# One core, attention into a gated MLP: a weight load in two, scores by two units earlier, two output copies on ScalarE, and gated work moved past unit 36

## The chip, the core and the metric

The kernel runs on one core of a Trainium2 chip. The metric is device time in microseconds: the median of several runs. Before the change it is 239.21 us (238.92, 239.21 and 239.23). TensorE (PE) multiplies matrices into eight PSUM banks, ScalarE (ACT) and VectorE (DVE) read these and write to SBUF, GpSimd (POOL) works on SBUF alone, and SyncE (SP) only issues transfers. Transfers are also issued from the queues of ACT and POOL.

## The reference

Grouped-query attention over 8 batches, whose output is the input of a gated MLP with a spatial mix over the 384 positions:

```python
k = np.repeat(k, group, axis=1); v = np.repeat(v, group, axis=1)   # 4 -> 16 heads
scores = scale * np.matmul(q, k.transpose(0, 1, 3, 2))              # 8 x 16 x 384 x 384
scores = scores - np.max(scores, axis=-1, keepdims=True)
attn = np.exp(scores)
attn = attn / (np.sum(attn, axis=-1, keepdims=True) + 1e-09)
x = np.matmul(attn, v)                                             # heads side by side: 8 x 384 x 1024
...
h = np.maximum(x @ w_in, 0.0)                                      # 1024 -> 1024
u, v = h[..., :512], h[..., 512:]
v_n = (v - mean(v)) / np.sqrt(var(v) + 1e-06)
v_s = np.einsum('ts,bsd->btd', w_spatial, v_n) + b_spatial[None, :, None]
return (u * v_s) @ w_out                                           # 512 -> 1024
```

All inputs and the output are float32. The kernel computes in float16 with float32 sums.

## The kernel before

**Two streams on one TensorE.** The kernel's order of instructions is written out by hand. The attention stream is a row of 144 units, 18 for each batch (`UNITS`). A unit is one block of 128 keys for one set of heads and queries; three units make a set, six sets a batch. `units` (L264) multiplies keys by queries into two PSUM banks for a unit (one for each half `hh`, the tile `sc`), and `exp` (L288) is two ScalarE activations from these to `aT`. When the three units of a set are done, `weigh` (L292) multiplies by v (tile `av`, 12 matmuls for a half), and VectorE takes the reciprocal of the sums and scales (`r`, `x`). For batch 0, x is transposed on TensorE (`x_turn`, L324, tile `xps`, copied by VectorE to `xt`); later batches send it through a transposing transfer on SyncE's queue (`x_send`, L334).

**The gated stream** is a generator (`gated`, L487). It yields the MLP's matmuls one by one, each with its cost: `v_part` (tile `pv`, eight matmuls of 512 columns), `u_part` (`pu`, 32 of 384), `s_part` (`psp`, 12 of 384) and `o_part` (`po`, four of 512 for each half of an output tile). It also yields marks `("from", n)`: nothing behind the mark may come before unit n. `pour` (L696) takes matmuls from it as long as some time is owed, and returns 0 at a mark that isn't reached. `o_part` copies each half from PSUM to `osb` on VectorE or ScalarE (`copy`, L214), and SyncE stores the whole.

**The main loops.** The first (L718 to 737) runs over units 0 to 20 (`ALONE`): one unit at a time up to unit `TWO` - 1, then two at a time; it carries out what `at(n, ...)` has put down for that unit (turns, casts, loads), then the `weigh` that is due, then pours as much gated work as the unit has to spare (`spare`, 736 ns, or 600 and 870 for two). The second (L743 to 765) runs over groups of three units from 21 on. Each has `share` of gated work, cut into four pieces (`F`) between scores, exponentials and `weigh`.

**Banks.** `bank` (L77) gives each tile the PSUM bank which, by a rough clock kept while the program is built, comes free first.

**Queues.** GpSimd's queue carries the loads that cast (`load_w_in`, L159, `load_w_out`) and several loads of q, k, v, in order among its casts (`cast_q`, L194; `cast_v`, L187; `cast_k`). SyncE's queue carries the other loads, the transposing sends (`k_send`, `q_send`, `x_send`) and the stores, in program order, each waiting there for what it needs. At L581 to 618 the first loads and casts are laid out, at L656 to 662 those of batch 2.

Of the kernel before, what the change touches and what calls it, by code (L numbers as in the profile page):

```python
# [17 lines left out]
def kernel(  # L18
# [51 lines left out]
    pool, dve, act, sp = nc.gpsimd, nc.vector, nc.scalar, nc.sync  # L70
# [14 lines left out]
    def spend(ns):  # L85
        clock[nc.tensor] += ns
# [42 lines left out]
    def load_q(b, j, eng=sp, ts=(0, 1, 2)):  # L129
        if ts[0] == 0:  # L130
            stage_tile("q", b, j)
        part_q(b, j, (0, 1), ts, eng)
# [26 lines left out]
    def load_w_in(half, lo, hi):  # L159
        cols = slice(half * DH, (half + 1) * DH)  # L160
        pool.dma_start(
            w_in16[:, lo:hi, cols],
            moe_w_in[lo * P : hi * P, cols].rearrange("(t p) f -> p t f", p=P),
        )
# [29 lines left out]
    def cast_q(b, j, eng, ts=None, hs=(0, 1)):  # L194
        if (b, j) not in q16s:
            q16s[b, j] = ld.tile([P, NT, G, 2, D], FP16, name=f"q16_{b}_{j}", tag="q16", bufs=4)
        t16 = q16s[b, j]
        src = stage["q", b, j].rearrange("p h t (r d) -> p h t r d", d=D)
        for hh in hs:
            if ts is None:  # L200
                eng.tensor_copy(t16[:, :, :, hh, :], src[:, hh])  # L201
            elif len(ts) > 1:
                t = slice(ts[0], ts[-1] + 1)
                eng.tensor_copy(t16[:, t, :, hh, :], src[:, hh, t])
            else:
                eng.tensor_copy(t16[:, ts[0], :, hh, :], src[:, hh, ts[0]])  # L206
# [249 lines left out]
    def o_part(b, tt, half):  # L456
        last = b == B - 1
        if half == 0:
            osbs[b, tt] = ops.tile([P, DM], FP32, name=f"osb_{b}_{tt}", tag="osb")
        osb = osbs[b, tt]  # L460
        rows = out[b].rearrange("(p t) d -> p t d", t=NT)

        parts = [(half * 512, 512, act if half and (last or tt == 1) else dve, sp)]
        if last and tt == NT - 1 and half:
            parts = [(512, 384, dve, sp), (896, 128, act, act)]
        for c0, width, eng, queue in parts:
            po = bank([P, 512], FP32, f"po_{b}_{tt}_{c0}")
            for m in range(NM):
                nc.tensor.matmul(  # L469
                    po[:, 0:width],  # L470
                    gTs[b][:, m, tt * P : (tt + 1) * P],
                    w_out16[:, m, c0 : c0 + width],
                    start=(m == 0),
                    stop=(m == NM - 1),
                )
                spend(C512 * width / 512)
                if m < NM - 1:
                    yield C512 * width / 512
            cols = slice(c0, c0 + width)
            copy(eng, osb[:, cols], po[:, 0:width], f"po_{b}_{tt}_{c0}")  # L480
            if last:
                queue.dma_start(rows[:, tt, cols], osb[:, cols])
            elif half:
                sp.dma_start(rows[:, tt, :], osb)
            yield C512 * width / 512
# [77 lines left out]
    def at(n, f, *args):  # L563
        todo.setdefault(n, []).append((f, args))
# [14 lines left out]
            nc.tensor.matmul(ps, zero16, zero16, start=True, stop=True)  # L579

    cast_k(0, pool, (0,), slice(1, 2))  # L581
    load_w_in(1, 0, 4)
    cast_k(0, dve, (0,), slice(0, 1))
    cast_q(0, 0, dve, (0,), (0,))
    cast_q(0, 0, dve, (0,), (1,))
# [13 lines left out]
    def behind_rest():  # L599
        load_q(1, 1, pool)  # L600
        load_v(1, pool)
        cast_q(0, 1, pool, (2,))
        load_w_in(0, 0, 4)
        load_w_in(0, 4, 8)
        new_spatial()
        pool.memset(spatial32["b"][:, 0:1], 0.0)
        pool.memset(spatial32["w"][:, 0, 0:1], 0.0)
        load_spatial(sp)
        cast_k(1, pool)
        load_k(2, pool)  # L610
        cast_q(1, 0, pool)
        load_q(2, 0, pool, (0,))
        cast_q(1, 1, pool, (0,))
        cast_q(1, 1, pool, (1, 2))
        load_q(2, 1, pool, (0,))
        cast_v(1, pool)
        cast_spatial()
        send_spatial()
# [34 lines left out]
    at(26, q_send, 2, 1, 0, 1)  # L653
    at(26, load_w_out, 0, DH)
    at(26, load_w_out, DH, DM)
    at(29, load_q, 2, 0, sp, (1, 2))  # L656
    at(29, load_v, 2)
    at(31, load_q, 2, 1, sp, (1, 2))
    at(36, cast_v, 2, pool)
    for j, n in ((0, 34), (1, 36)):  # L660
        at(n, cast_q, 2, j, pool, (1, 2))
        at(n + 1, q_send, 2, j, 1, NT)
# [25 lines left out]
    STEP = (NT * NK * C512 + NM * NK * C384 + NM * NT * C384 + 6 * NM * C512) / SETS  # L688
# [7 lines left out]
    def pour(n, owed):  # L696
        while owed > 0:
            if n < wait_for[0]:
                return 0.0
            x = next(fill, None)  # L700
            if x is None:
                return 0.0
            if isinstance(x, tuple):
                wait_for[0] = x[1]
            else:
                owed -= x
        return owed
# [6 lines left out]
    F = (0.2, 0.3, 0.1, 0.4)  # L714
    owed = 0.0
    halves = {}
    TWO = 13
    for u in range(ALONE):  # L718
        if u < TWO or (u - TWO) % 2 == 0:
            pairs = units(u, 1)  # L720
            if u >= TWO and u + 1 < ALONE:
                pairs += units(u + 1, 1)
            for pair in pairs:
                exp(*pair)
        spare = 736 if u < TWO else (600 if (u - TWO) % 2 == 0 else 870)
        for f, args in todo.pop(u, []):
            f(*args)
            spare -= 224 if f in (q_turn, x_turn, k_turn) else 0
        for b, s in ends.pop(u, []):
            halves.setdefault(u, []).append((b, s, 0))  # L730
            halves.setdefault(u + (0 if s == 0 else 1), []).append((b, s, 1))
        for h in halves.pop(u, []):
            weigh(*h)
            spare -= 372
            if h[2]:
                turn_x(*h[:2], u)
        owed = pour(u, min(owed, 0) + spare)
    for u in sorted(halves):
        for h in halves[u]:
            weigh(*h)  # L740
    owed = 0.0
    late = [(b, s, hh) for u in (ALONE, ALONE + 1) for b, s in ends.pop(u, []) for hh in range(2)]
    for n in range(ALONE, total, NT):  # L743
        share = STEP * (0.85 if n < 90 else 1.0)
        exps = units(n, NT)
        for pair in exps[:NT]:
            exp(*pair)
        owed = pour(n, owed + share * F[0])
        for h in late:
            weigh(*h)  # L750
            if h[2]:
                turn_x(*h[:2], n)
        owed = pour(n, owed + share * F[1])
        for u in range(n, n + NT):
            for f, args in todo.pop(u, []):
                f(*args)
        for pair in exps[NT:]:
            exp(*pair)
        owed = pour(n, owed + share * F[2])
        late = []  # L760
        for u in range(n, n + NT):
            for b, s in ends.pop(u + 2, []):
                weigh(b, s, 0)
                late.append((b, s, 1))
        owed = pour(n, owed + share * F[3])
# [36 lines left out]
```

## Time and profile before

| What | us |
|---|---|
| median of three runs | 239.21 |
| the profiled execution | 238.38 |
| its span (first to last instruction) | 236.4 |
| TensorE busy | 230.1 |
| ScalarE busy | 169.5 |
| VectorE busy | 142.7 |
| GpSimd busy | 101.5 |
| first scores on TensorE | 5.74 |
| first group of three units (21 to 23) | 27.56 |
| last `av`, then gated work alone | 202 |

Times within the program are us from the start of the span. Busy time of TensorE is taken from modelled ends, since matmuls are pipelined: the start of one matmul to the start of the next is the better measure, and the prediction uses it. The other engines' rows have real starts and durations. The granted TensorE clock is 1.00 in every stretch. The share of the DMA engines is about 1.1 from 6 to 85 us and falls behind that to 0.8 and below.

### The profile page before, as it was taken

What the parts mean: (1) busy time and instruction counts of PE and PEld (TensorE: products, weight loads), DVE (VectorE), ACT (ScalarE), POOL (GpSimd) and SP (SyncE); (2) the same over time, 40 slices, a digit from 0 to 9 for tenths busy, and PEclk for the clock granted to TensorE, in tenths of its full rate; (3) what the DMA queues carried; (4) which work ended last, traced back from release to release, by engine and by line L of the source; (5) the groups of instructions that cost most, each with busy time, mean ns of one, the idle gap of its engine ahead of it and who ended that gap; (6) DMA issues with size and microseconds to landing.
All of it is one profiled execution on the core that took longest, in us unless ns stands there. A gap on an engine that the chain in (4) does not pass through costs nothing.

```text
span 236.4 us, 5917 instructions
## 1 busy us (share of the span) xinstructions
PE 230.1 (97%) x2312; PEld 123.6 (52%) x2312; DVE 142.7 (60%) x379; ACT 169.5 (72%) x348; POOL 101.5 (43%) x145
## 2 busy tenths in 40 slices
PE   7899999999999999999999999999999999999993
PEld 6455655545554546544564545555465455545541
DVE  2568774676457764566646576376744667367362
ACT  2999989969997869977797776986697776401211
POOL 3669583651464543275045800575022500460550
PEclk9999999999999999999999999999999999999999
DMA  6999979999998999899989899389912643240147
GB/s 196 273 305 320 272 143 178 212 266 260 259 227 208 260 372 192 228 200 318 193 239 224 234 202 302 63 281 158 257 26 44 114 155 89 49 177 0 68 200 267
DMA packets 67467, 47.47 MB, mean 201 GB/s; under 512 B 48336, under 2 KB 60416, under 8 KB 67440
## 3 DMA queue, kind: packets, MB, share of 16 engines
q1 hardware_dynamic: 62512, 39.86, 69.4%
q0 software_dynamic: 3952, 6.42, 12.2%
q10 hardware_dynamic: 976, 0.82, 1.1%
q8 instruction: 18, 0.29, 0.5%
q14 instruction: 9, 0.07, 0.1%
HBM read 25.95 MB, written 12.58 MB: 163 GB/s over the span
## 4 chain that ended last, share of the span: by engine, by line
PE 93%; DVE 2%; DMA 2%; issue 0%; ACTq 0%; ACT 0%
PE pu L412 18%; PE pv L353 18%; PE po L469 18%; PE sc L278 15%; PE av L298 15%; PE psp L431 7%; DMA q<-in_q_dram 2%; PE qps L238 1%; PE xps L330 1%; DVE x L313 1%; DVE osb L216 1%; DVE qT L216 0%; DVE q L206 0%; DVE r L311 0%; DVE vr L367 0%
## 5 line engine op out<-in xcount | busy, mean ns | idle before, releaser
L290 ACT ACTIVATE aT<-sc 128x512 f16<-128x512 f32 x288 | 147.7, 612 | 31.0 <-PE sc L278 30.3
L298 PEld LDWEIGHTS <-aT 128*128 128x128 f16 x1152 | 47.0, 97 | 17.0 <-issue 2.1
L353 PE MATMUL pv<-w_in,xt 128*128 128x512 f16 x192 | 51.0, 380 | 0.1
L298 PE MATMUL av<-v,aT 128*128 128x65 f16 x1152 | 50.5, 193 | 0.0
L469 PE MATMUL po<-w_out,gT 128*128 128x512 f16 (+2 forms) x196 | 50.5, 375 | 0.0
L412 PE MATMUL pu<-xt,w_in 128*128 128x384 f16 x256 | 49.9, 326 | 0.0
L397 POOL TENSOR_SCALAR vn<-vr,rstd,nmr 128x512 f16<-128x512 f32 x23 | 17.7, 783 | 66.7 <-DVE nmr L392 45.3
L448 POOL TENSOR_TENSOR gT<-vs,uT 128x384 f16<-128x384 f32 x31 | 32.5, 1058 | 31.8 <-DVE r L311 16.9
L313 DVE TENSOR_TENSOR x<-av,r 128x256 f16<-128x256 f32 x96 | 40.7, 424 | 3.3
L278 PE MATMUL sc<-qT,kT 64*128 64x512 f16 x288 | 41.6, 380 | 0.4 <-DVE qT L216 0.2
L311 DVE RECIPROCAL r<-av 128x4 f32<-128x4 f32 x96 | 17.1, 179 | 40.4 <-PE av L298 40.1
L216 DVE COPY osb<-po 128x512 f32<-128x512 f32 (+1 forms) x39 | 26.6, 683 | 17.3 <-PE po L469 17.2
L412 PEld LDWEIGHTS <-w_in 128*128 128x128 f16 x256 | 22.1, 98 | 17.1 <-issue 5.5
L423 ACT ACTIVATE uT<-pu 128x384 f16<-128x384 f32 x32 | 15.8, 495 | 16.0 <-PE pu L412 15.8
L469 PEld LDWEIGHTS <-gT 128*128 128x128 f16 x196 | 17.4, 98 | 17.3 <-issue 3.2
L353 PEld LDWEIGHTS <-xt 128*128 128x128 f16 x192 | 15.8, 97 | 17.8 <-issue 6.0
L278 PEld LDWEIGHTS <-kT 64*128 64x128 f16 x288 | 10.9, 94 | 23.7 <-issue 12.1
L431 PE MATMUL psp<-wsT,vn 128*128 128x384 f16 x96 | 22.2, 327 | 0.0
L443 DVE TENSOR_TENSOR vs<-psp,bias_bc 128x384 f32<-128x384 f32 x32 | 17.6, 552 | 7.0 <-PE psp L431 6.9
L201 POOL CAST q<-q 128x768 f16<-128x768 f32 x22 | 17.6, 831 | 9.2 <-DMA q<-in_q_dram 4.5
L367 DVE TENSOR_SCALAR vr<-pv 128x512 f32<-128x512 f32 x24 | 16.4, 683 | 8.4 <-PE pv L353 8.3
L379 DVE BATCH_NORM_STATS2 stats<-vr 128x6 f32<-128x512 f32 x24 | 16.4, 685 | 0.1
(47 smaller groups left out, 98.9 us busy)
## 6 DMA issues: line engine op xcount, KB each, us to landing
out_dram<-osb SPq DMA_DIRECT2D x21, 512.0 KB, 3.2
q<-in_q_dram SPq DMA_DIRECT2D x10, 768.0 KB, 5.8
v_None<-in_v_dram SPq DMA_DIRECT2D x6, 384.0 KB, 5.8
w_in<-in_moe_w_in_dram POOLq DMA_DIRECT2D x4, 512.0 KB, 9.8
k_None<-in_k_dram SPq DMA_DIRECT2D x5, 384.0 KB, 4.0
q<-in_q_dram POOLq DMA_DIRECT2D x2, 768.0 KB, 8.4
out_dram<-osb SPq DMA_DIRECT2D x5, 256.0 KB, 2.2
w_out<-in_moe_w_out_dram POOLq DMA_DIRECT2D x2, 512.0 KB, 8.5
```

The source lines that it names most:

```text
L201: eng.tensor_copy(t16[:, :, :, hh, :], src[:, hh])
L216: (act.copy if eng is act else dve.tensor_copy)(o, i)
L278: nc.tensor.matmul(sc, kTs[b][rows, j, kt * P : (kt + 1) * P], qTs[b, j][rows, qt].rearrange("p (r i c) -> p i r c", r=G, i=G), start=True ...
L290: act.activation(a, sc, AF.Exp, scale=scale)
L298: nc.tensor.matmul(av[:, i * (D + 1) : (i + 1) * (D + 1)], aT[:, kt, hh, i * P : (i + 1) * P], v1[b % 2][:, 2 * j + hh, kt, 0 : D + 1], st ...
L313: dve.tensor_tensor(x16s[b][:, qt, c : c + 256].rearrange("p (i d) -> p i d", i=G), o[:, :, 0:D], r.to_broadcast([P, G, D]), ALU.mult,)
L353: nc.tensor.matmul(pv, xts[b][:, kt, st * P : (st + 1) * P], w_in16[:, kt, DH:DFF], start=(kt == 0), stop=(kt == NK - 1),)
L397: (dve if b == 0 and st == 1 else pool).tensor_scalar(vn, v_r.pop((b, st)), rstd[:, st : st + 1], nmr[:, st : st + 1], op0=ALU.mult, op1=A ...
L412: nc.tensor.matmul(pu[:, 0:S], w_in16[:, kt, m * P : (m + 1) * P], xts[b][:, kt, :], start=(kt == 0), stop=(kt == NK - 1),)
L431: nc.tensor.matmul(psp[:, 0:S], v_n[b, st][:, m * P : (m + 1) * P], wsT16[:, st, :], start=(st == 0), stop=(st == NT - 1),)
L448: pool.tensor_tensor(gT, vs, uT, ALU.mult)
L469: nc.tensor.matmul(po[:, 0:width], gTs[b][:, m, tt * P : (tt + 1) * P], w_out16[:, m, c0 : c0 + width], start=(m == 0), stop=(m == NM - 1),)
```

## The change

Six edits. The first load of w_in's second half of columns is issued as two transfers. Units go by two from unit 11 instead of 13. In the first loop the transposes of x are put down behind the gated work poured for that unit. Two copies of output halves, (batch 0, tile 1, half 0) and (batch 1, tile 0, half 0), go from VectorE to ScalarE. In groups that start before unit 36 the share of gated work is 0.8 of a step instead of 0.85. And the loads and casts of q and v are moved: the cast of batch 1's first q in two with a load between, v of batch 2 loaded before q on SyncE's queue and cast at unit 33 instead of 36.

```diff
-        parts = [(half * 512, 512, act if half and (last or tt == 1) else dve, sp)]
+        by_act = half and (last or tt == 1) or (b, tt, half) in ((0, 1, 0), (1, 0, 0))
+        parts = [(half * 512, 512, act if by_act else dve, sp)]
...
-    load_w_in(1, 0, 4)
+    load_w_in(1, 0, 2)
+    load_w_in(1, 2, 4)
...
-        cast_q(1, 0, pool)
+        cast_q(1, 0, pool, (0,))
         load_q(2, 0, pool, (0,))
+        cast_q(1, 0, pool, (1, 2))
...
+    at(29, load_v, 2)
     at(29, load_q, 2, 0, sp, (1, 2))
-    at(29, load_v, 2)
     at(31, load_q, 2, 1, sp, (1, 2))
-    at(36, cast_v, 2, pool)
+    at(33, cast_v, 2, pool)
...
-    TWO = 13
+    TWO = 11
...
+        turns = []
         for f, args in todo.pop(u, []):
-            f(*args)
+            if f is x_turn:
+                turns.append(args)
+            else:
+                f(*args)
             spare -= 224 if f in (q_turn, x_turn, k_turn) else 0
...
         owed = pour(u, min(owed, 0) + spare)
+        for args in turns:
+            x_turn(*args)
...
-        share = STEP * (0.85 if n < 90 else 1.0)
+        share = STEP * (0.8 if n < 36 else 0.85 if n < 90 else 1.0)
```

## The prediction

> **What bounds the kernel now.** I read the page's summary and its chain of waits first, then the timeline of the stages that the diff touches, then the wait before each long gap of the chain.
>
> ```profile
> PE 230.1 (97%) x2312; PEld 123.6 (52%) x2312; DVE 142.7 (60%) x379; ACT 169.5 (72%) x348; POOL 101.5 (43%) x145
> ...
> PE 93%; DVE 2%; DMA 2%; issue 0%; ACTq 0%; ACT 0%
> ```
>
> TensorE is the chain, and the granted clock is 1.00 throughout, so a gain must be TensorE time. I took the start-to-start times of its matmuls: a 512-column one follows another after 216 ns, a 384-column one after 162, the narrow `av` ones after 29. What lies above these, and above 0.32, 0.54 and 0.75 us for blocks of two, four and six `sc` (from the first to the next other matmul), is lost: behind the first loads 0.54 us at 10.5 to 11.4, 0.18 at 22 to 23, 0.73 at 27.6 to 31.9, 0.10 at 54.1, 0.60 at 54.4, 0.09 at 69.0, 0.16 at 80.8, 0.12 at 100.1, 0.15 at 205.2: 2.7 us. No gain but a saved switch can be larger.
>
> The switch: from 16.36 a `pv` of 216 ns is followed by `sc` only after 0.31 us, and `sc` by `av` after 0.32 us instead of 0.216.
>
> ```profile
> 16.36 0.38 PE L353 MATMUL pv<-w_in,xt 128*128 128x512 f16 x1
> 16.67 0.39 PE L278 MATMUL sc<-qT,kT 64*128 64x512 f16 x2
> 16.99 0.54 PE L298 MATMUL av<-v,aT 128*128 128x65 f16 x12
> ```
>
> So each block of scores costs 0.09 + 0.10 = 0.19 us beyond its columns. ScalarE is as tight here: its row runs without a gap.
>
> ```profile
> 6.15 15.32 ACT L290 ACTIVATE aT<-sc 128x512 f16<-128x512 f32 x30 [1.34 <-PE sc L278]
> ...
> 21.70 6.11 ACT L290 ACTIVATE aT<-sc 128x512 f16<-128x512 f32 x12 [0.23 <-PE sc L278]
> ```
>
> The largest later loss, and the stage that causes it (the second view is of busy time by stretch: us, PE, PEld, DVE, ACT, POOL, clock, DMA):
>
> ```profile
> 54.42 1.30 PE L278 MATMUL sc<-qT,kT 64*128 64x512 f16 x6
> ...
> 54.68 0.10 PEld L278 LDWEIGHTS <-kT 64*128 64x128 f16 x2 [0.17 <-DVE x L313]
> ...
> 55.13 0.10 PEld L278 LDWEIGHTS <-kT 64*128 64x128 f16 x2 [0.36 <-issue]
> ```
>
> ```profile
> 47.90:52.07 4.17, 4.17 (x43) 2.03 (x42) 3.07 (x8) 3.05 (x6) 2.82 (x5) 1.00 1.06 294
> 52.07:54.41 2.34, 2.34 (x34) 1.34 (x33) 1.13 (x6) 1.85 (x4) 0.35 (x1) 1.00 1.15 133
> ```
>
> This block of six takes 1.35 us to the next work (55.77) instead of 0.75. The 0.10 before it is the last `av` waiting for its exponential. The group before is only 2.34 us long, against six exponentials of 0.51 us (3.05): the gated stream had stopped at its "not before unit 42" mark, so the scores of unit 42 came before ScalarE had emptied their PSUM banks.
>
> **The change, part by part.**
>
> **Units by two from 11.** Units 11 and 12 share one block: one switch fewer, -0.19 us. The shares 600 + 870 replace 2 x 736, and I add up the owed sum: units 10, 11, 12 get 1, 1, 2 `pv` instead of 1, 2, 1, and every later unit as before. ScalarE follows, because its gap of 0.23 at 21.70 is a wait for `sc`: it has 0.23 to give, 0.19 is taken.
>
> **x turned behind gated work.** Only where the unit pours something does the order change. By the same sums units 5, 9, 15 and 18 pour nothing at their end, so only unit 12 differs: four transposes (4 x 56 ns) go behind two `pv` (432 ns). `x` of its second half would be finished about 0.3 us after the transposes' old place in the new order (`av` 0.37, reciprocal 0.18 and multiply 0.42 on VectorE); the two `pv` hide it. Cost 0, and 0.3 without that cover.
>
> **Less gated work up to unit 36.** One share is 2916 ns; 0.05 of it in four groups (24 to 33; at 21 the stream stands at its mark) is 583 ns. Stepping through the shares matmul by matmul, the old order comes out as in the trace, and the new one is three `pv` (648 ns) behind at the end of group 36 and catches all of it up in group 39, which pours six `pv` instead of three. From unit 42 the order is the same. No work goes away; group 39 grows from 2.34 to 2.99 us, about the 3.05 that ScalarE needs, so the 0.60 and the 0.10 should close: -0.70. What is late next: the groups of units 27 and 30 shrink by 0.32 and 0.16 us. The first holds 4.17 us of ScalarE work in 4.41, so it is full: between 0 and +0.2; I take +0.1.
>
> **Two copies on ScalarE.** Rows: VectorE 0.69 us, ScalarE 0.59 to 0.64. The copy of (1,0,0) is what holds the bank here:
>
> ```profile
> 80.44 0.67 DVE L216 COPY osb<-po 128x512 f32<-128x512 f32 x1
> 80.78 0.10 PEld L298 LDWEIGHTS <-aT 128*128 128x128 f16 x1
> 81.16 0.52 PE L298 MATMUL av<-v,aT 128*128 128x65 f16 x12
> ```
>
> ScalarE idles 1.01 us before 80.07, so there the copy is done by about 80.25: -0.16. The copy of (0,1,0) meets a ScalarE with 3.70 us of 4.16; with 0.64 it is 4.34, and runs 0.2 into group 54, which has 3.04 of 4.07. Its own loss of 0.09 at 69.0 may go; the `av` of group 54, 0.75 us behind its exponentials now, would stand about level with them. -0.1 to +0.3; I take 0.
> The Trainium skill (ScalarE: Activation LUTs, Rules for kernel authors) speaks against such a move: simple element work belongs on VectorE, and ScalarE costs about 0.3 us plus 0.83 ns per element, an estimate of 0.72 us here. This trace disagrees for a copy out of PSUM (0.59 to 0.64 beside 0.69); by the page the sum would be 0.1 us worse at most.
>
> **First w_in load in two.** One more GpSimd issue of 0.75 us (row at 8.20), put into GpSimd's idle 4.57 to 7.03, where it waits for k; the second load still issues at 8.20. The first half is needed at 13.01 and landed, whole, at 12.19 by the landing events. Cost 0; if the cover went, see the last rival.
>
> **Third v sooner, cast_q split.** The split adds 0.32 us of GpSimd (two casts of 0.38 and two of 0.585 for 1.60) ahead of a 2.48 us wait for the spatial weights: 0. `v` of batch 2 was cast until 49.95, needed at 50.54; the new order needs it at about 50.1, so the move protects 0.2 us. Its price: on SyncE v (384 KB) goes before q, so q lands near 49.0 instead of 47.84; on GpSimd the cast of v stands before the cast of q. The cast of q (1.17) then ends near 50.0 (was 49.07), and behind it in SyncE's queue stand q's transposing send (49.09, now 50.0, 1.23 us of issue), `x_send` of batch 1's last third (50.78, now 51.2), k and q loads of batch 3. `x_send` landed 3.84 us after issue: 55.1; its `pv` would come at 54.9 (55.77 less 0.19, 0.70). Bounds: 0 (`x_send` as early as now) to +1.2 (v as late as now, 49.0, both casts behind it, `x_send` landing at 56.1); v, issued first, should land 1 to 2 us before that, so +0.2.
>
> **Sum.** -0.19 - 0.70 - 0.16 + 0.1 + 0 + 0.2 = -0.75. The profiled execution took 238.38 (span 236.4 and 2.0 around it), 0.8 under the median of 239.21. Off the median: **238.5 us**.
>
> **Rivals.**
>
> **Loads take the gain (239.3).** For: the DMA share is 1.0 and more up to 85 us, so landings don't follow TensorE; q of batch 3 landed at 70.59 for scores at 71.52, and its slack of 0.93 falls to 0.18. Against: `x_send` issues earlier when x is earlier. If v lands at 49.0, the `pv` of unit 42 waits 1.2: -0.95 without its term becomes +0.2, and the rest is lost there. Chance 0.18.
>
> **More goes (237.8).** ScalarE's 0.1 and SyncE's 0.2 don't arise, and of the 0.73 at 27.6 to 31.9 (transposes and scores that wait for banks) some 0.3 goes, as the planner gives the banks out anew: -1.35. Against: nothing in the diff aims there. Chance 0.12.
>
> **The back half of w_in comes late (239.8).** Mechanism: GpSimd's queue carries one more transfer ahead of the load of k tiles 4 to 7; that load landed at 16.25 and its first `pv` started at 16.36, a slack of 0.11. If a hole as between the w_out issue (33.37) and its first packet (34.83), 1.46 us, opens between the halves, TensorE stands still 1.35 us there: +1.35 - 0.75 = +0.6. It decides from a landing past about 17.1. Against: the packets of that queue began at 7.41, long after the issue, behind the other loads, so a hole of issue is covered. Beside it, the Trainium skill (DMA: Bandwidth & Descriptors, Anatomy of one DMA, and Rules for kernel authors) gives each such transfer a fixed 2.0 us and advises fewer, larger ones; taken serially that would be a stall of 1.9 us, and about 240.3. The trace, with transfers landing 1.2 to 2.4 us apart under load, shows them overlapped. Chance 0.13.
>
> **That nothing changes** because order and banks stay is ruled out by the sums above.
>
> **How the numbers follow.** Forecast 238.5, chance 0.57, its own range 238.1 to 238.9. What a measurement of this kernel can tell from no change is about 0.2%, 0.48 us: faster means under 238.73. Faster: 0.47 of the 0.57, all 0.12, 0.03 of the 0.18: 0.62. Slower (above 239.69): 0.12 of the 0.13 and 0.05 of the loads, where they cost 0.3 more: 0.17. Within: 0.21. Range over all: 237.8 to 239.7.
>
> **What would show it.** Right: scores of units 11 and 12 as one row of four near 16.7; group 39 near 3.0 us, and six scores after it in 0.8; no gap before `av` near 80. Wrong: a gap before `pv` at 16.4, before `pv` of unit 42 (near 55), or before the scores of unit 54 (near 70.8, where q lands), or new bank waits on ScalarE in groups 27 to 33 and 51 to 54.

## The result, and the profile after

The changed kernel takes **239.50 us** (median of 22 runs, 238.47 to 242.06). The kernel before, run beside it on the same chip, takes 238.77 (22 runs, 237.98 to 240.37). The ratio is 1.0042, with a 95% interval of 1.0026 to 1.0058: 1.0 us slower by the ratio and 0.73 by the two medians, where 0.75 us faster was forecast. The ratio leaves out the one run after, 242.06, that is over 1.5% above the fastest of its kernel. The median of 239.21 from which the forecast was counted came from three runs; 22 put it at 238.77, so 0.4 us of the distance between 238.5 and a sum made on 238.77 is the starting point. The sign is not.

It is no even shift. The lowest runs lie 0.5 us apart, but 7 of the 22 runs after are above 240 us, against 2 of 22 before.

And part of it lies outside the span. Device time is the span, from the first instruction to the last, and what lies around it. In the 111 runs of the kernel before whose spans are on record (those of the experiments), 1.96 to 2.14 us lie around the span; in the changed kernel it is 2.42 by the median, and over 2.2 in 18 of its 22 runs. So some 0.4 us of the loss is no wait of TensorE, and no row of a timeline shows it: the instructions of the trace all lie within the span.

The profiled execution of the changed kernel took 239.24 (span 236.8), 0.86 above that of before. First its summary: busy time of each engine, and the shares of the chain of waits by engine.

```profile
PE 229.8 (97%) x2312; PEld 123.8 (52%) x2312; DVE 141.6 (60%) x377; ACT 170.0 (72%) x350; POOL 102.5 (43%) x148
...
PE 87%; DMA 9%; POOL 1%; DVE 1%; SPq 1%; issue 0%
```

TensorE has the same 2312 matmuls. But it was 93% of the chain, and is 87%; transfers went from 2% to 9%. So transfers now stand where TensorE waits, though a share of the chain isn't a price. To place and price the waits, I take the start of the first scores of each unit and subtract the same start in the profile before (negative is sooner; units in `exp` order):

| unit, start before | 10, 15.41 | 11, 16.67 | 13, 18.98 | 36, 47.90 | 39, 52.08 | 45, 59.13 | 51, 67.35 | 54, 71.52 | 63, 83.92 | last, 197.29 |
|---|---|---|---|---|---|---|---|---|---|---|
| after | -0.48 | +0.07 | -0.14 | -0.57 | -0.79 | -0.06 | -0.06 | +0.50 | +0.48 | +0.49 |

A lead of 0.48 from sooner first loads is lost before unit 11; 0.21 is won by unit 13; between units 27 and 39 scores run ahead, as gated work is poured later; by unit 45 that is paid back, and more; before unit 54 0.56 goes at one stroke. Nothing happens behind unit 63. The places, in the timeline of the changed kernel (start, us, engine, line, operation, output<-inputs, count, in brackets the idle time before and what ended it):

```profile
16.43 0.38 PE L353 MATMUL pv<-w_in,xt 128*128 128x512 f16 x1 [0.39 <-DMA w_in<-in_moe_w_in_dram]
16.74 0.60 PE L278 MATMUL sc<-qT,kT 64*128 64x512 f16 x4
...
54.19 1.07 PE L278 MATMUL sc<-qT,kT 64*128 64x512 f16 x6
55.70 0.61 PE L353 MATMUL pv<-w_in,xt 128*128 128x512 f16 x2 [0.43 <-DMA xt<-x]
...
72.02 0.82 PE L278 MATMUL sc<-qT,kT 64*128 64x512 f16 x6 [0.54 <-DMA qT<-q]
...
81.64 0.53 PE L298 MATMUL av<-v,aT 128*128 128x65 f16 x12
```

At 16.43 the first `pv` that needs the second w_in load stands still, and 0.55 us go between units 10 and 11 (its load landed at 16.39, at 16.25 before). At 16.74 units 11 and 12 do share a row of four `sc`. From 54.19 the six scores of unit 42 take 1.51 us to the next work, not 0.75; the timeline puts the last part of that down to `x_send`'s transfer. At 72.02 the scores of unit 54 wait for batch 3's q.

Busy time by stretch for groups 36 and 39 (us, PE, PEld, DVE, ACT, POOL, clock, DMA share, GB/s), to be read against the 4.17 and 2.34 of before:

```profile
47.33:51.29 3.96, 3.96 (x42) 1.93 (x43) 2.68 (x8) 3.05 (x6) 2.15 (x4) 1.00 0.95 310
51.29:54.19 2.90, 2.90 (x37) 1.67 (x37) 1.85 (x5) 2.42 (x6) 1.18 (x2) 1.00 0.82 122
```

Group 39 grew to 2.90, as forecast (2.99). What stood behind the forecast's +0.2 is seen in SyncE's queue, before and then after (start, duration of the issue):

```profile
42.77 1.46 SPq L122 DMA_DIRECT2D q<-in_q_dram  x1
44.29 0.45 SPq L112 DMA_DIRECT2D v_None<-in_v_dram  x1
...
49.09 1.23 SPq L256 DMA_TRANSPOSE qT<-q  x1
50.78 1.23 SPq L337 DMA_TRANSPOSE xt<-x  x1
```

```profile
42.77 1.44 SPq L112 DMA_DIRECT2D v_None<-in_v_dram  x1
44.27 0.49 SPq L122 DMA_DIRECT2D q<-in_q_dram  x1
...
50.31 2.10 SPq L256 DMA_TRANSPOSE qT<-q  x1
52.51 1.25 SPq L337 DMA_TRANSPOSE xt<-x  x1
```

q of batch 2 lands at 49.06 instead of 47.84, its two casts on GpSimd start at 49.11 instead of 47.90, so the transposing send starts 1.22 later, and its issue takes 2.10 instead of 1.23. The send of x behind it starts 1.73 later and lands at 55.65 (54.62 before). The q load of batch 3 is issued at 55.81 (54.55 before), and its transposed tile lands at 71.88, not 70.58: scores at 71.52 before had 0.94 to spare. (Times of landing are the trace's landing events.)

### The profile page after: what moved, and what is told of

Its sections match the earlier page's. It is cut to its first block, busy times and chain, and to the rows that moved or that the text cites. A ratio compares the mean times of both kernels' runs of the same rounds, so it can differ in the third digit from the quotient of the medians.

```text
span 236.8 us, 5923 instructions
## 1 busy us (share of the span) xinstructions
PE 229.8 (97%) x2312; PEld 123.8 (52%) x2312; DVE 141.6 (60%) x377; ACT 170.0 (72%) x350; POOL 102.5 (43%) x148
## 4 chain that ended last, share of the span: by engine, by line
PE 87%; DMA 9%; POOL 1%; DVE 1%; SPq 1%; issue 0%
PE pu L412 18%; PE pv L353 18%; PE po L470 17%; PE sc L278 14%; PE av L298 13%; PE psp L431 7%; DMA w_in<-in_moe_w_in_dram 4%; DMA qT<-q 2%; DMA v_None<-in_v_dram 2%; DMA xt<-x 1%; POOL q L201 1%; PE qps L238 1%; DVE osb L216 1%; PE xps L330 0%; SPq L112 0%
## 5 line engine op out<-in xcount | busy, mean ns | idle before, releaser
L353 PE MATMUL pv<-w_in,xt 128*128 128x512 f16 x192 | 51.2, 380 | 0.8 <-DMA xt<-x 0.4
L216 DVE COPY osb<-po 128x512 f32<-128x512 f32 (+1 forms) x37 | 25.2, 682 | 15.4 <-PE po L470 15.4
L470 PEld LDWEIGHTS <-gT 128*128 128x128 f16 x196 | 17.5, 98 | 17.0 <-issue 2.7
L443 DVE TENSOR_TENSOR vs<-psp,bias_bc 128x384 f32<-128x384 f32 x32 | 17.5, 551 | 6.7 <-PE psp L431 6.5
L201 POOL CAST q<-q 128x768 f16<-128x768 f32 x20 | 16.0, 831 | 8.8 <-DMA q<-in_q_dram 4.2
L216 ACT COPY osb<-po 128x512 f32<-128x512 f32 (+1 forms) x12 | 6.8, 567 | 13.9 <-PE po L470 13.9
```

The source lines that it names most:

```text
L216: (act.copy if eng is act else dve.tensor_copy)(o, i)
L353: nc.tensor.matmul(pv, xts[b][:, kt, st * P : (st + 1) * P], w_in16[:, kt, DH:DFF], start=(kt == 0), stop=(kt == NK - 1),)
L470: nc.tensor.matmul(po[:, 0:width], gTs[b][:, m, tt * P : (tt + 1) * P], w_out16[:, m, c0 : c0 + width], start=(m == 0), stop=(m == NM - 1),)
```

## The experiments

**Theory A**, as it stood after the result: the two moves (v loaded before q, v cast at unit 33) make q late, and with it SyncE's queue. **Theory B**: the smaller share of gated work up to unit 36 makes it, by the longer group 39. **Theory C**: the split of w_in, at the start. Some expectations below give the letter B to another rival, that landings do not follow TensorE and take any gain; each says what it means by it. All kernels compute everything. Medians stand beside the runs of the kernel before on the same chip (238.68, 238.65, 238.31 and 238.50 us for the four groups, 23 to 35 runs each). "Shift" is the table's measure: first scores less those of before, from one profiled execution.

| kernel | median us | ratio [95%] | shift at 10 | 13 | 36 | 39 | 45 | 54 | 63 |
|---|---|---|---|---|---|---|---|---|---|
| after | 239.50 | 1.0042 [1.0026, 1.0058] | -0.48 | -0.14 | -0.57 | -0.79 | -0.06 | +0.50 | +0.48 |
| e1 after without the moves | 239.43 | 1.0041 [1.0010, 1.0071] | -0.10 | +0.11 | +0.13 | +1.26 | +1.58 | +1.48 | +1.32 |
| e2 moves alone | 239.78 | 1.0042 [1.0013, 1.0072] | -0.58 | -0.45 | -0.45 | -0.45 | -0.45 | -0.45 | -0.45 |
| e3 share alone | 238.67 | 0.9994 [0.9976, 1.0012] | +0.12 | +0.12 | -0.31 | -0.39 | -0.07 | -0.07 | -0.08 |
| e4 split, units by two, x turn, cast_q | 239.19 | 1.0019 [0.9986, 1.0052] | -0.37 | -0.22 | -0.21 | -0.21 | -0.21 | -0.22 | -0.22 |
| e5 split alone | 239.11 | 1.0021 [0.9998, 1.0044] | -0.82 | +0.73 | +0.73 | +0.73 | +0.73 | +0.73 | +0.73 |
| e6 v before q alone | 239.84 | 1.0064 [1.0039, 1.0089] | 0.00 | 0.00 | +0.03 | +0.75 | +0.76 | +0.75 | +0.75 |
| e7 cast at 33 alone | 240.02 | 1.0064 [1.0039, 1.0089] | +1.35 | +1.35 | +1.35 | +1.35 | +1.66 | +2.47 | +2.47 |
| e8 after without split and moves | 238.54 | 0.9993 [0.9967, 1.0020] | +1.55 | +1.39 | +0.98 | +1.31 | +1.63 | +1.53 | +1.37 |
| e9 after, again | 239.43, one run | none | +0.08 | +0.11 | -0.31 | -0.52 | -0.04 | +0.92 | +0.76 |
| e10 v behind q, cast on VectorE | 239.98 | 1.0070 [1.0039, 1.0100] | -0.32 | -0.20 | -0.62 | +0.88 | +1.19 | +1.10 | +0.94 |
| e11 without split, moves, share | 238.30 | 0.9991 [0.9965, 1.0017] | -0.35 | -0.51 | -0.51 | -0.51 | -0.51 | -0.60 | -0.76 |
| e12 e11, w_in's second load sooner | 240.38 | 1.0049 [1.0014, 1.0084] | +0.93 | +0.77 | +0.78 | +0.78 | +0.77 | +0.68 | +0.52 |
| e13 after with the old share | 239.08 | 1.0019 [1.0000, 1.0038] | -0.33 | -0.49 | -0.48 | -0.48 | +0.12 | +0.53 | +0.37 |
| e14 moves alone, again | 240.05, one run | none | +0.65 | +0.77 | +0.76 | +0.78 | +1.56 | +1.68 | +1.68 |
| e15 after, q's send behind x_send | 240.82 | 1.0115 [1.0078, 1.0152] | +0.11 | +0.34 | -0.07 | -0.29 | +2.59 | +2.50 | +2.34 |
| e16 e11, again | 238.23 | 0.9993 [0.9976, 1.0009] | -0.88 | -0.94 | -0.92 | -0.92 | -0.92 | -1.02 | -1.18 |

Two cautions on reading it. The shift at unit 10 is mostly not the edits': kernels that are the same there differ by up to 2.4 us (e8 and e16), as first loads land sooner or later. And a profiled execution is one draw: e2's was the lowest of its 12 runs, e8's the highest. So rows are read as differences along the row; for what a kernel costs, the ratio counts. The ratio holds one thing that no row shows: around the span, after, e1, e8, e9, e11, e12, e13 and e16 spend 2.33 to 2.45 us by the median, and all others 1.96 to 2.05, as the kernel before does. All that the traces have behind the span is one packet of 8 KB of an instruction queue. It starts 2.19 or 2.20 us after the span's end in these eight, and 1.74 to 2.03 in the others (none in e15). So a load of instructions at the program's end goes with the 0.4 us; that it is the cause is not shown. The eight have the two copies on ScalarE, but so have e10 and e15.

### Each part alone, and after without the moves

e1 undoes, in the changed kernel, the order and the unit:

```diff
+    at(29, load_q, 2, 0, sp, (1, 2))
     at(29, load_v, 2)
-    at(29, load_q, 2, 0, sp, (1, 2))
-    at(33, cast_v, 2, pool)
+    at(36, cast_v, 2, pool)
```

> The changed kernel with v of batch 2 loaded and cast where it was before. Theory A (the order of v and q on SyncE's queue): q of batch 2 lands near 47.8 again, its send leaves at about 49, the pv of unit 42 waits under 0.2 us, the scores of unit 54 don't wait; the 0.56 to 0.73 us ahead at units 39 to 42 is kept to the end: 0.7 to 0.9 us under the kernel before. Theory B (landings that do not follow TensorE take any gain): the scores of unit 54 start at 71.5 to 71.9 again, and the time is within 0.3 us of the kernel before.

The wait at 54 went, as Theory A said, but no time came back. One wait took the other's place: v's cast stands behind q's, and `av` of batch 2 stands still for it. Timeline of e1:

```profile
49.91 1.17 POOL L204 CAST q<-q 128x512 f16<-128x512 f32 x2 [2.17 <-DMA q<-in_q_dram]
...
51.14 0.83 POOL L189 CAST v<-v_None 128x768 f16<-128x768 f32 x1
52.02 0.52 PE L298 MATMUL av<-v,aT 128*128 128x65 f16 x12 [1.18 <-POOL v L189]
```

Here q landed at 49.86 and v at 51.02, each 2.0 us later than before, with issues at 42.55 and 43.19, no later than before's. So the wait is the order's and the late landing's together. Both forecasts of e1's time missed: it is 0.41% over the kernel before.

e2 makes the same two moves in the kernel before, and nothing else:

```diff
+    at(29, load_v, 2)
     at(29, load_q, 2, 0, sp, (1, 2))
-    at(29, load_v, 2)
...
-    at(36, cast_v, 2, pool)
+    at(33, cast_v, 2, pool)
```

> The kernel before with v of batch 2 loaded before q and cast at unit 33, nothing else. Theory A: q lands 1.2 us later, the send of q and the x_send behind it leave over 1 us later, and the scores of unit 54 wait, since the transposed q of batch 3 lands near 71.9 against 71.5: 0.3 to 0.6 us over the kernel before. Theory B: the order of two loads is indifferent, within 0.15 us of the kernel before.

Theory A holds for the cost of the moves alone: +0.42%, 1.0 us, more than the 0.3 to 0.6 expected. Its profile, though, is its best run, 237.99, and shows no wait. The late kind is e14, the same kernel (below).

e3 is the line of the share alone:

```diff
-        share = STEP * (0.85 if n < 90 else 1.0)
+        share = STEP * (0.8 if n < 36 else 0.85 if n < 90 else 1.0)
```

> The kernel before with the share 0.8 up to unit 36, nothing else. If the loss of 0.70 us at 54.1 to 55.8 was the short group of units 39 to 41: that group 3.0 us long, no wait in the scores of unit 42, and 0.5 to 0.7 us under the kernel before, as the scores of unit 54 had 0.9 us of slack. Theory B: the pv of unit 42 or the scores of unit 54 wait for a landing instead, within 0.2 us of the kernel before.

The smaller share is not the loss, and the forecast's -0.70 falls with it: from unit 21 to unit 45 the row wins 0.19, and the median does not move. The rival had the time right, but no landing is waited for there. Windows of e3 for groups 36 and 39, columns as above, and then its timeline:

```profile
47.59:51.69 4.10, 4.10 (x43) 1.93 (x43) 2.82 (x8) 3.05 (x6) 2.14 (x4) 1.00 1.14 327
51.69:54.57 2.88, 2.88 (x37) 1.66 (x36) 1.72 (x5) 2.40 (x5) 1.17 (x2) 1.00 1.21 137
```

```profile
52.17 4.52 ACT L290 ACTIVATE aT<-sc 128x512 f16<-128x512 f32 x9 [1.06 <-PE sc L278]
...
54.31 0.69 DVE L367 TENSOR_SCALAR vr<-pv 128x512 f32<-128x512 f32 x1 [0.22 <-PE pv L353]
54.57 0.11 PEld L278 LDWEIGHTS <-kT 64*128 64x128 f16 x4
54.57 1.07 PE L278 MATMUL sc<-qT,kT 64*128 64x512 f16 x6
...
55.06 0.10 PEld L278 LDWEIGHTS <-kT 64*128 64x128 f16 x2 [0.38 <-issue]
...
55.13 0.42 DVE L313 TENSOR_TENSOR x<-av,r 128x256 f16<-128x256 f32 x1
...
55.70 0.81 PE L353 MATMUL pv<-w_in,xt 128*128 128x512 f16 x3
```

Group 39 lasts 2.88 us, as the sum of shares has it, yet the six scores behind it still take 1.13 us to the next work instead of 0.75: of the 0.60, 0.37 stays. Which engine they wait for is seen from what ends just before each start. In the kernel before they waited three times. The second score waited 0.25 until an exponential of ScalarE ended, at 54.63. The fourth waited 0.24 until VectorE had read `pv` out of its bank (`vr`), and the `pv` behind the scores 0.11 until VectorE had read `av` (`x`):

```profile
54.40 0.68 DVE L367 TENSOR_SCALAR vr<-pv 128x512 f32<-128x512 f32 x1
...
55.20 0.42 DVE L313 TENSOR_TENSOR x<-av,r 128x256 f16<-128x256 f32 x1
```

In e3 the first of these is gone and the other two are left, 0.25 and 0.12: the fourth score starts at 55.06, 0.05 us behind the end of `vr` at 55.00, and `pv` at 55.70, 0.15 behind that of `x` at 55.55. The 0.05 between `vr` and the fourth score is the same in 17 of the 18 profiles (not in e15, where q comes last). The `av` that waited 0.10 waits no more, but at 50.37 another waits 0.14 for v's cast, which leaves 0.19.

e4 makes the edits of the start alone: the split, `TWO = 11`, the turns of x behind the poured work, and batch 1's cast of q in two:

```diff
+    load_w_in(1, 0, 2)
+    load_w_in(1, 2, 4)
...
+        cast_q(1, 0, pool, (0,))
...
+    TWO = 11
...
+        for args in turns:
+            x_turn(*args)
```

> The kernel before with the four edits of the first 28 us alone (w_in's first load in two, units by two from 11, x turned behind gated work, the cast of q in two). Theory: one switch of 0.19 us less, 0.05 of it lost to ScalarE: 0.1 to 0.2 us under the kernel before; if k and q land 0.45 us sooner again (6.5 and 6.7 instead of 7.0 and 7.2), the pv of unit 10 waits about 0.5 us for w_in's second load near 16.4 and nothing of it is kept. Rival: the sooner landing was chance, k and q land at 7.0 and 7.2, no wait at 16.4, and the same 0.1 to 0.2 us.

The lead of 0.37 goes at unit 10, where `pv` waits for the w_in load (landed 16.31); then 0.21 is won. The interval of its ratio is too wide to tell e4 from before. e5 is the split alone:

```diff
-    load_w_in(1, 0, 4)
+    load_w_in(1, 0, 2)
+    load_w_in(1, 2, 4)
```

> The kernel before with w_in's first load issued as two, nothing else. Theory C (the split lets GpSimd's transfers go ahead of q's third load on ScalarE's queue): that load lands at 10.7 instead of 9.7 in many executions, GpSimd's cast and all its loads behind are 1 us late, and executions of 240 to 241 us appear: median 0.4 us or more over the kernel before. Theory A (only the order of v and q matters): within 0.15 us, range as before (237.7 to 240.4).

Timeline of e5:

```profile
7.38 0.76 POOL L161 DMA_DIRECT2D w_in<-in_moe_w_in_dram  x1
...
17.09 0.38 PE L353 MATMUL pv<-w_in,xt 128*128 128x512 f16 x1 [1.39 <-DMA w_in<-in_moe_w_in_dram]
```

The second load is issued 0.82 sooner than before (8.20) and lands 0.80 later, at 17.05 (16.25): 1.55 us of TensorE at unit 10. That is the place of the forecast's rival of the back half of w_in, in this execution. The ratio is 0.2% above before, with an interval that just includes no change, and 2 of its 12 runs are above 240 us, against 4 of the 24 of before beside it. Theory C's own reason is not seen: q's third load on ScalarE's queue landed at 8.85, sooner than the 9.69 of before.

The 18 profiles together say more of the split. Six of the eight that have it (after, e1, e4, e5, e10, e15) show a wait of 0.17 us or more for this load before `pv`; none of the ten without it does, though e2 and e16 start as soon. From issue to landing the load took 8.5 to 9.7 us with the split, and 8.0 to 8.9 in the nine without it that issue it at the same place.

### The two moves apart, and after without split and moves

e6 changes only the order of the two loads, with the cast left at unit 36; e7 only the unit of the cast, with the loads as before. Of e2's diff, e6 has the first three lines and e7 the last two:

```diff
-    at(36, cast_v, 2, pool)
+    at(33, cast_v, 2, pool)
```

> The kernel before with v of batch 2 loaded before q; the cast of v stays at unit 36. Theory A: q lands 1.2 us later and with it its cast and send; that is the whole of the 0.4% of both moves together: 0.6 to 1.1 us over the kernel before. Rival: the cast at unit 33 did it: within 0.2 us.

> The kernel before with the cast of v at unit 33, the loads as before. Theory A': GpSimd waits there for v (landing 49.0) before it casts q (landed 47.8), so q's send is 1.2 to 2 us late as well: 0.5 to 1.1 us over the kernel before. Rival: the cast's place alone costs nothing, within 0.2 us.

Each half alone costs +0.64%, 1.5 us (7 and 6 runs), more than either expectation. In e6 v lands first (47.90) but is cast last, behind a q that lands at 49.25. Timeline of e6:

```profile
49.30 1.17 POOL L204 CAST q<-q 128x512 f16<-128x512 f32 x2 [2.05 <-DMA q<-in_q_dram]
...
50.41 0.83 POOL L189 CAST v<-v_None 128x768 f16<-128x768 f32 x1
51.30 0.52 PE L298 MATMUL av<-v,aT 128*128 128x65 f16 x12 [0.56 <-POOL v L189]
```

In e7 GpSimd stands 1.71 us before v's cast, with q's cast, long possible, behind it: q had landed at 49.03. Then `pv` waits 0.35 for `xt` at 57.42, and the scores of unit 54 wait 0.55 for q. Timeline of e7:

```profile
50.31 0.82 POOL L189 CAST v<-v_None 128x768 f16<-128x768 f32 x1 [1.71 <-DMA v_None<-in_v_dram]
51.08 1.17 POOL L204 CAST q<-q 128x512 f16<-128x512 f32 x2
```

So either move alone sets one tile's cast behind the other's landing. That the two together cost less is not shown (+0.42%, with an interval to 0.72).

e8 is after with both taken out (the x turn, units by two, copies, share and cast_q stay):

```diff
-    load_w_in(1, 0, 2)
-    load_w_in(1, 2, 4)
+    load_w_in(1, 0, 4)
...
     at(29, load_q, 2, 0, sp, (1, 2))
+    at(29, load_v, 2)
...
+    at(36, cast_v, 2, pool)
```

> The changed kernel without the split of w_in's load and without the moves of v: units by two from 11, x turned behind gated work, q's cast in two, two copies on ScalarE, share 0.8. If split and moves are the causes: no executions above 239.5, and 0.5 to 0.9 us under the kernel before. Theory B (transfers that don't follow TensorE): late executions as in the changed kernel, 0.3 to 1 us over the kernel before.

It is level with before, and not 0.5 to 0.9 us under it; 3 of its 12 runs are above 239.5. So what the changed kernel loses lies in the split and the moves. e1 differs from e8 by the split alone and costs 0.41%, so the moves are not all of it; the changed kernel without the split alone was not run. By its span e8 wins: 236.15 us by the median, 0.45 under the runs of before beside it, and 0.41 of that goes around the span. Its profile has, as e1's, v landing at 51.07 and a wait of 0.56 for its cast; it is the highest of its 12 runs.

### Other ways to keep the gain

e9 is the changed kernel itself, with no edit, for a second profile.

> The changed kernel as it is, a second profile. Theory A: again the transposed q of batch 3 lands over 1 us later than the first scores of unit 54 want it beside the kernel before, and TensorE waits 0.3 us or more for xt near 55 or for q near 71. Rival (the first profile was a chance): no wait over 0.2 us at either place.

The changed kernel's second profile has the same two places, `xt` at 55.7 and q at 72.4, and its lead of 0.77 at unit 3 is likewise gone by unit 11 (+0.32). Timeline of e9:

```profile
55.72 0.60 PE L353 MATMUL pv<-w_in,xt 128*128 128x512 f16 x2 [0.19 <-DMA xt<-x]
...
72.44 0.82 PE L278 MATMUL sc<-qT,kT 64*128 64x512 f16 x6 [0.53 <-DMA qT<-q]
```

e10 takes v's cast out of GpSimd's queue, with the loads in the old order:

```diff
-    at(33, cast_v, 2, pool)
+    at(36, cast_v, 2, dve)
```

> The changed kernel with q loaded before v again, and v of batch 2 cast on VectorE at unit 36 instead of GpSimd at unit 33, so that neither cast stands before the other. Theory A: the send of q leaves about 1.2 us after q lands, as in the kernel before; av of batch 2 waits under 0.2 us, xt near 55 under 0.2, no wait at unit 54: from unit 27 on 0.3 us or more ahead of where the changed kernel is, and 0.2 to 0.6 us under the kernel before. Theory B: the lead at unit 36 is lost at the next landing all the same: within 0.3 us of the kernel before.

No wait at 54 (qT landed 69.73): q's lateness is the moves'. But VectorE's queue is in order too, and v, landed at 48.90, was cast 2.1 us after that, last behind the copy of an output half. The expectation of under 0.2 us for this wait missed. Timeline of e10:

```profile
50.44 0.66 DVE L216 COPY osb<-po 128x512 f32<-128x512 f32 x1
51.01 0.55 DVE L189 CAST v<-v_None 128x768 f16<-128x768 f32 x1
51.62 0.54 PE L298 MATMUL av<-v,aT 128*128 128x65 f16 x12 [1.53 <-DVE v L189]
```

e11 makes four edits in the kernel before: units by two, the x turn, cast_q in two, and the two copies. e16 is the same kernel once more.

```diff
+        by_act = half and (last or tt == 1) or (b, tt, half) in ((0, 1, 0), (1, 0, 0))
+        parts = [(half * 512, 512, act if by_act else dve, sp)]
...
+        cast_q(1, 0, pool, (0,))
...
+    TWO = 11
...
+        for args in turns:
+            x_turn(*args)
```

> The kernel before with units by two from 11, x turned behind gated work, q's cast in two and the two copies on ScalarE; no split, no moves of v, share 0.85. The terms that the profiles bear out: 0.15 at units 11 to 21, 0.09 at 69 and 0.16 at 80.8, none of it waiting for a landing: 0.3 to 0.5 us under the kernel before. Rival: the 0.15 makes x_send overtake the load of w_out, v and q of batch 2 land 1 to 2 us later and more is lost there: no gain or slower.

> The kernel of e11 once more, for its time: its profile showed 0.16 us won at units 11 to 13 and 0.25 at 69 to 81 and nothing lost behind. If that holds in most executions: 0.2 to 0.5 us under the kernel before. If the scatter of the first loads hides it: within 0.2 us.

Between units 11 and 13 e11 wins 0.16 and e16 0.21 (e16 had lost 0.15 of its lead just before); both win 0.09 to 0.10 before unit 54 and 0.16 before 63, and lose nothing behind. The ratios, 0.09% and 0.07% under before, do not leave the noise. The spans show where the expected 0.3 to 0.5 went: they are 236.0 and 235.95 us by the median, 0.3 and 0.45 under those of before beside them (236.3 and 236.4), and 0.37 and 0.31 of that is lost around the span. Shares of e16's chain, then its timeline:

```profile
PE 94%; DVE 3%; DMA 1%; issue 0%; SPq 0%
```

```profile
15.94 0.61 PE L278 MATMUL sc<-qT,kT 64*128 64x512 f16 x4
...
79.32 0.82 PE L470 MATMUL po<-w_out,gT 128*128 128x512 f16 x3
79.98 0.53 PE L298 MATMUL av<-v,aT 128*128 128x65 f16 x12
```

Transfers are back at 1% of the chain. `av` follows its `po` at 79.98 0.66 us after it, three matmuls of 216 ns with no gap: the bank is free in time.

e12 is e11 with w_in's second load issued right behind the first:

```diff
     load_w_in(1, 0, 4)
+    load_w_in(1, 4, 8)
...
-    load_w_in(1, 4, 8)
```

> The kernel of e11 with w_in's second load issued right behind the first, ahead of GpSimd's wait for v. Theory D (w_in's second load is the wall of the first 17 us): it lands 1 us or more sooner (near 15), pv of unit 10 never waits for it, and the starts that are 0.4 to 0.8 us sooner are kept: another 0.3 us or more under e11. Rival: the DMA engines are full there, so q's last thirds come that much later and scores of unit 12 or the cast before them wait: no gain over e11.

It was issued at 4.54 and landed at 16.16: against e11 (7.84 and 15.79) 3.3 us sooner in and 0.4 later out, against before 0.1 sooner out. In its place SyncE's load of q landed late (15.00; e11 12.27, before 13.19) and stopped VectorE, and TensorE behind it. Timeline of e12:

```profile
15.02 0.49 DVE L206 CAST q<-q 128x256 f16<-128x256 f32 x2 [1.57 <-DMA q<-in_q_dram]
...
16.12 0.28 PE L330 MATMUL xps<-ident,x 128*128 128x128 f16 x2 [1.15 <-DVE x L313]
```

### What in the changed kernel pays for the moves

e13 is after with the old share:

```diff
-        share = STEP * (0.8 if n < 36 else 0.85 if n < 90 else 1.0)
+        share = STEP * (0.85 if n < 90 else 1.0)
```

> The changed kernel with the share 0.85 again; the moves of v and q, the split and the rest stay. If the moves cost by themselves: q lands near 49 and its send leaves near 50.3, the transposed q of batch 3 near 71.5 to 72 against scores at 71.3: a wait of 0.2 to 0.6 us there, and 0.2 us or more over the kernel before. If they cost only together with the smaller share: no wait at 54 over 0.2 us, and 0.2 to 0.5 us under the kernel before.

Both waits are there without the smaller share. Over the profiles, `pv` waits for `xt` and the scores of unit 54 for q in after, e7, e9, e13 and e14, five of the six that cast v at unit 33 and send q as after does; neither wait is in the eleven that cast it at unit 36. Timeline of e13:

```profile
55.88 0.82 PE L353 MATMUL pv<-w_in,xt 128*128 128x512 f16 x3 [0.64 <-DMA xt<-x]
...
72.04 0.82 PE L278 MATMUL sc<-qT,kT 64*128 64x512 f16 x6 [0.43 <-DMA qT<-q]
```

> The moves of v and q alone, a second profile. Theory A: measured against its own scores of unit 36, the transposed q of batch 3 lands 0.4 us or more later than in the kernel before; a wait at unit 54 of 0 to 0.6 us. Rival: no such shift in the landings; the lost time lies in the first 17 us, where executions differ anyway.

e14 is e2's kernel in a late execution. Against e2's row 1.23 us are the start's; 0.78 more goes between units 39 and 45, where `pv` waits 0.82 for `xt` (landed 57.27), and 0.12 before 54. v landed at 49.44 and q at 50.79, 2.3 us later than in e2.

e15 changes where q's transposing send stands, so that x's goes first:

```diff
-        at(n + 1, q_send, 2, j, 1, NT)
+        at(n + (3 if j == 0 else 1), q_send, 2, j, 1, NT)
```

> The changed kernel with the send of batch 2's first q rest put behind x_send on SyncE's queue (todo of unit 37 instead of 35). Theory A: x_send leaves near 50, xt lands near 53.5, the pv of unit 42 doesn't wait (0.5 us less there); the transposed q then lands near 55 and the scores of unit 42 wait for it about as long: no gain, within 0.3 us of the changed kernel. Rival: the wait at 54.9 alone is the loss: 0.4 us or more under the changed kernel.

`xt` did land sooner, at 55.05. But q's send came 3.3 us later than in after, behind the load of k and its long issue, and the scores of unit 42 waited for it. Timeline of e15:

```profile
50.27 1.23 SPq L337 DMA_TRANSPOSE xt<-x  x1
51.61 1.94 SPq L112 DMA_DIRECT2D k_None<-in_k_dram  x1
53.64 2.78 SPq L256 DMA_TRANSPOSE qT<-q  x2
...
57.60 0.82 PE L278 MATMUL sc<-qT,kT 64*128 64x512 f16 x6 [2.84 <-DMA qT<-q]
```

I had taken the send of q as free for two units: a miss. Each of the two orders tried in this queue makes one tile late.

**Over all runs**, executions above 240 us are 9 of 133 for the kernel before, 1 of 48 for the kernels with neither split nor moves (e3, e8, e11, e16), and 7 of 22, 5 of 12, 5 of 12, 3 of 12 and 2 of 12 for after, e1, e2, e4 and e5, which have one or both; e13, with both, has 1 of 12. The variants have more: 3 of 7 and 3 of 6 for e6 and e7, 6 of 12 for e10, 7 of 12 for e12, all 6 for e15.

## Why the prediction was wrong

**The step that turned the sign: third v sooner.** The step said that q lands near 49.0, the send starts at 50.0, `x_send` at 51.2, and took +0.2 from bounds of 0 to +1.2. q landed at 49.06 and the send started at 50.31, so the chain up to there was nearly right. What was mis-sized is what follows: the send's issue took 2.10 and not 1.23, `x_send` started at 52.51, and `pv` of unit 42 waited 0.38 for it beyond the 0.11 that VectorE takes there anyway. And the k and q loads of batch 3, which the step named behind `x_send`, were put at nothing: q's later load cost 0.56 at unit 54. That is 0.9 for 0.2 in one execution; alone the moves cost 1.0 us by the ratio (e2). The rival "loads take the gain" named both places, but it priced only the first, and its 0.18 was too low for a queue whose slack of 0.93 at unit 54 it had itself reduced to 0.18 by the gain, and not by q's later load as well (issued 1.26 later). That its 239.3 is close to 239.5 is in part luck: it stood on 239.21, and 0.4 of the measured time lies around the span.

**What failed in size: less gated work.** -0.70 and +0.1 came out as -0.19 alone (e3). The pouring went as stepped through, and group 39 as long as forecast. The step that failed is "about the 3.05 that ScalarE needs, so the 0.60 and the 0.10 should close": it put the whole 0.60 down to banks that ScalarE had not emptied. ScalarE's part was 0.25, and it closed, as did the 0.10. The rest was VectorE's, which reads `pv` and `av` out of their banks, and 0.37 stays with the group at 2.88. The +0.1 in groups 27 and 30 did not arise; 0.14 for v's cast did.

**First w_in load in two: cost 0.** Not 0. The idle stretch of GpSimd did cover the issue, but the second load landed at 16.39, 16.31 and 17.05 (after, e4, e5) with issues at 7.71, 7.83 and 7.38, sooner than the 8.20 of before. In the changed kernel 0.55 us is lost at unit 10; 0.37 of it (the lead of 0.48 less the slack of 0.11) would have been lost with before's landing of 16.25 too, so the landing of 16.39 itself is worth some 0.14 to 0.18. e5 puts the edit alone at +0.2% [-0.02, +0.44]. The rival for this place had the right tile, and 1.55 for its 1.35 in one execution. Its mechanism is not what happened: in after, e4 and e5 the packets of GpSimd's queue follow one another up to 17.5 us with no gap over 0.13, so no hole opens between the halves. That it is the split and not only the sooner starts follows from the count over the profiles (six waits of eight against none of ten); why it makes the second load later stays open.

**Put at nothing: what lies around the span.** The sum took "2.0 around it" as fixed. It is 2.42 in the changed kernel, 0.4 us that no step of the forecast looked at.

**Right.** Units by two: one row of four scores at 16.74 (forecast near 16.7), -0.21 for -0.19 (-0.16 in e11). The x turn: nothing lost. The copies: -0.16 at 80 as worked out (units 60 to 63 in e9, e11, e13 and e16), and the one of (0,1,0), taken at 0 between -0.1 and +0.3, won 0.09 at unit 54 in e11 and 0.10 in e16. The copy on ScalarE takes 0.59 in this trace, as in the rows of before; the rule of the Trainium skill (ScalarE: Activation LUTs, Rules for kernel authors) weighed in the prediction, whose 0.3 us is given for a bias by pointer, is not borne out for this move. cast_q in two: nothing seen in the traces.

**The parts do not add.** After costs 0.42%, without the moves 0.41 (e1), with the old share 0.19 (e13), without moves and split nothing (e8). Removing one wait can uncover the next: v's cast behind q's where the moves are undone (TensorE idles 1.18 us there in e1, 0.39 in e8). Leads are not always lost: e2, e11 and e16 keep theirs of 0.45 to 0.94 from unit 13 to the end. That the moves and the split carry the loss within the span rests on e2, e5 to e8, e11 and e16, and on e1 beside e8; how much of it is each one's cannot be told from ratios that are 0.2 to 0.3% uncertain.

**Open.** Which edit brings the 0.4 us around the span, and how. Why in e1, e8 and e14 q and v landed some 2 us late: in these three w_out's second load landed at 47.4 to 47.6, in all the other profiles at 43.4 to 46.0. Its issue was late there (35.26, 36.09 and 35.77, before 34.11), but e15's was as late (36.15), and its q and v landed only 0.4 later than those of after. And why the first loads scatter: that belongs to no edit here.

## What to carry to other kernels

Before an in-order queue is reordered, follow every instruction behind the moved one to what it feeds, to the last consumer, and compare each slack with the whole delay, with issue times taken from the most crowded stretch and not the least. Before a wait is put down to one engine, look at what ended just before each start in it: 0.35 of the 0.60 here was another engine's, and the edit could not reach it. A lead that is won ahead of a landing that comes no sooner is lost there. And take device time apart into the span and what lies around it, or a gain within the span (e11, e16) goes unseen.

## What the hardware showed that was not expected

**A load issued sooner did not land sooner.** In 17 profiles w_in's second load was issued at 7.07 to 8.86 and landed 8.0 to 9.7 us later, at 15.59 to 17.09. Issued at 4.54 (e12) it took 11.6 and landed at 16.16, 0.1 us sooner than in before, while SyncE's load of q landed 1.8 later. The Trainium skill (DMA: Bandwidth & Descriptors, Issuing engines are not separate DMA queues) states that transfers started by ScalarE, SyncE and GpSimd run interleaved on the same 16 DMA engines whichever of them started them; that GpSimd's sooner transfer made one of SyncE's late agrees.

**The issue of a transposing transfer on SyncE isn't of fixed length.** From 42 to 56 us in the kernel before it took 1.23 or 1.24 us each time; it took 2.10 in the changed kernel at 50.31, and 4.30 in e14 at 43.48, and all that SyncE has behind it waits as long.

**One program on one core scatters by 3 us from run to run.** Of 133 executions of the kernel before, 132 took 237.66 to 240.62 us and one 241.87, and e2 and e14, one program, differ by 1.23 us at unit 10 already. A sum of steps of 0.1 to 0.2 us is checked along the rows of traces, not by three runs.

**The time around the span isn't fixed.** It was 1.96 to 2.14 us in all 111 recorded runs of the kernel before, and 2.25 us or more in 18 of 22 of the changed one. In the eight profiles with the longer time a packet of instructions starts 2.19 or 2.20 us behind the span's end, in the nine others that have one 1.74 to 2.03.
